# K and V read in 2 MB blocks instead of 1 MB blocks, in the first three passes of an attention and dense forward and backward kernel

## The chip, the cores and the metric

The kernel runs on one core of one Trainium2 chip. The metric is the time of one execution on the device, in microseconds (us); lower is better. The state of a run says whether it fell into a disturbed, slower execution. Medians are quoted with their range.

The engines are called as in the profile: PE multiplies matrices (PEld are its weight loads), DVE does vector work, ACT does activations and copies, POOL does general work and SP only issues DMA transfers here. A core has 16 DMA engines. PSUM is the memory that PE's results go to. The granted clock is the share of its full speed that PE was allowed, as the profile records it.

## The reference, cut to what matters

The program is one decode step (a single token) through two pairs of attention and dense layer, with the gradients of everything. The attention layers share one cache of keys and values.

```python
# Hq, Hkv, Sk, Dh = 32, 4, 65536, 128     k_cache, v_cache: 64 MB each, bfloat16
def _A_ref(x, k_cache, v_cache, wq, wo):
    q = ...(x @ wq)
    scores = einsum(q, k) * Dh ** -0.5
    p = softmax(scores); o = einsum(p, v)
    return o @ wo
def _B_ref(x, w1, b1, w2, b2):            # w1: 1024 x 3584, w2: 3584 x 1024
    h = relu(x @ w1 + b1); return (h * h) @ w2 + b2
x = x + _A_ref(_layernorm(x), ...); x = x + _B_ref(_layernorm(x), ...)   # twice
# outputs: x, and by jax.vjp the gradients of x, k_cache, v_cache, wq, wo, w1, b1, w2, b2
```

Almost all of the data is the cache. It is read in four passes: forward of the first attention layer, forward of the second, backward of the second, and a last pass that does the rest of the backward work and writes the two cache gradients.

## The kernel before, where the change and the argument touch it

The slots. K and V blocks, weight slabs and staging for stores share 12 buffers of 1 MB (later also the buffers of `E`, the exponentials of the scores). A slot is given back with a time stamp and the one given back longest ago is taken first. The clock of these stamps, `NOW["step"]`, is one per step of a pass, plus 0.01 for each slot given back. All of this happens while the program is built; on the chip only the result exists, as instructions that wait for the last readers of the slot they overwrite.

```python
BLK = J * DH                                   # J = 32 keys of 128 elements: 8 KB per partition
FREE = [(0, i) for i in range(NSLOT)]          # NSLOT = 12, kept sorted by time
NOW = {"step": 0}

class Slot:
    def __init__(self, name, fill=False):
        n = 0
        if fill:                               # used by stores and a few others
            ready = [k for k, (at, _) in enumerate(FREE) if at <= NOW["step"] - 1]
            n = ready[-1] if ready else 0
        self.i = FREE.pop(n)[1]
        ...

def give_slot(i, more=0):
    NOW["step"] += 0.01
    insort(FREE, (NOW["step"] + more, i))

def kv8(t, g, c8):                             # 8 columns of keys; loads their block at first touch
    b, j = divmod(c8, J)
    key = (t, g, b)
    if key not in KV["have"]:
        sl = Slot("blk_" + t)
        v = sl.t[:, :].rearrange("p (j d) -> p j d", d=DH)
        nc.sync.dma_start(out=v, in_=KVIN[t][g][b])
        KV["have"][key] = (sl, v)
    return KV["have"][key][1][:, j:j + 8, :]
```

Between two passes lies a dense stretch, in which layer weights stream through the same slots.

A forward pass. For each group of eight K columns, PE transposes them (`kT`), ACT or DVE copies the result out of PSUM as a K tile (`kt`), PE multiplies it with the query (`kS`), and after 128 columns ACT does eight exponentials. The V product follows 23 steps behind.

```python
def kT(g, c8):
    kb8 = kv8("k", g, c8)
    ...                                        # 8 transposes into PSUM
    evac(kt[:, :, :], pt[:, :, :])             # K tile: by ACT or DVE, whichever has less to do
def stats(g, su):                              # every 128 columns
    ...
    for h in range(R):                         # R = 8 exponentials on ACT
        nc.scalar.activation(out=E(g, c0, SU)[:, :, L["lr"].start + h], in_=S[:, h, :], func=ACTF.Exp, ...)
def v8(g, c8): ...                             # V product with E
FWD_LAG = TLEAD + SU // 8 + 5                  # TLEAD = 2, SU = 128
pipeline(items, [(kT, 0), (kS, TLEAD), (v8, FWD_LAG)], bg, end)
```

## Time and profile before

The median of three runs was 2037.67 us (2037.56 to 2038.18).

I cut the span into stages by the first and last matmul of each pass that reads a K or V block. The next fence is the view of time windows of the kernel before, one line for a stage: passes one, two, three and four are lines 1, 3, 5 and 7, and the dense stretches between them are lines 2, 4 and 6. Columns: window, its length, then busy us (and instructions) of PE, PEld, DVE, ACT and POOL, the granted clock of PE, the busy share of the 16 DMA engines, and GB/s.

```profile
12.50:377.90 365.40, 296.27 (x6656) 280.57 (x6657) 168.10 (x387) 175.40 (x387) 0.29 (x1) 0.93 1.01 411
377.90:433.30 55.40, 44.03 (x818) 42.43 (x815) 22.07 (x61) 13.68 (x15) 0.55 (x11) 0.85 0.87 328
433.30:781.00 347.70, 285.42 (x6586) 270.65 (x6584) 165.89 (x382) 173.71 (x385) 0.29 (x1) 0.93 1.01 407
781.00:833.30 52.30, 39.67 (x786) 36.66 (x784) 24.32 (x66) 18.09 (x23) 0.48 (x9) 0.85 0.87 330
833.30:1197.50 364.20, 296.44 (x6509) 265.68 (x6506) 170.96 (x327) 151.06 (x186) 0.67 (x1) 0.96 1.01 412
1197.50:1255.70 58.20, 51.56 (x932) 48.51 (x929) 41.40 (x105) 34.63 (x40) 0.48 (x10) 0.84 0.82 299
1255.70:2012.90 757.20, 663.08 (x8376) 393.38 (x8376) 581.20 (x1201) 526.81 (x1011) 85.25 (x158) 0.91 0.97 399
```

In the three first passes the DMA share is 1.01, while PE is busy about four fifths of the time and DVE and ACT less than half. So the loads set the pace there. In the dense stretches the share is still 0.82 to 0.87.

The next lines are two windows of 50 us inside passes one and three of the kernel before, the same columns. They show the rate of a full stretch, 410 to 417 GB/s in nearly all such windows.

```profile
150.00:200.00 50.00, 42.21 (x957) 39.91 (x955) 24.40 (x53) 25.23 (x53) 0.00 (x0) 0.93 1.01 416
1100.00:1150.00 50.00, 39.20 (x823) 35.19 (x822) 23.43 (x40) 21.57 (x30) 0.00 (x0) 0.93 1.02 414
```

```profile
SPq L351 <- PE ps_mv L397: 36.8, 15, 11.4
```

### The profile page before, as it was taken

The page shows a single profiled execution, that of the slowest core. Times are in us where ns is not written, and L with a number is a line of the kernel's source. Part 1 is how long each engine was busy: PE and PEld are TensorE (multiplying, and loading weights), DVE is VectorE, ACT ScalarE, POOL GpSimd, SP SyncE. Part 2 cuts the span into 40 slices and gives each one's busy share as a digit, 9 for nine tenths or more (in the row PEclk, how much of TensorE's full clock was granted, in tenths as well). Part 3 has the DMA queues.
Part 4 walks back from the last instruction along what each step waited for, and adds up shares of the span by engine and source line. Part 5 has one row for each costly group of instructions (what it writes and reads, how often), then busy time and mean ns, then how long its engine had stood idle before and what let it go on. Part 6 is the DMA issues. An engine that isn't in the chain of part 4 may idle for free.

```text
span 2035.9 us, 69009 instructions
## 1 busy us (share of the span) xinstructions
PE 1689.3 (83%) x30754; PEld 1344.3 (66%) x30754; DVE 1188.6 (58%) x2586; ACT 1103.0 (54%) x2063; POOL 92.4 (5%) x232
## 2 busy tenths in 40 slices
PE   7888887688788886887978888979988978898897
PEld 6778777688787776776867777545544545454454
DVE  4444454255444542555464446867967877687775
ACT  3544454255444542445354345767766766576675
POOL 0000000000000000000000000101101111010111
PEclk9999899799899996999999988988988998698898
DMA  9999999999999998999999986999999999999995
GB/s 384 416 410 414 413 414 415 360 335 406 411 414 413 413 415 323 398 415 410 416 412 414 416 338 231 375 424 393 422 424 424 423 423 404 423 415 423 423 371 212
DMA packets 136536, 803.50 MB, mean 395 GB/s; under 512 B 12448, under 2 KB 12462, under 8 KB 52398
## 3 DMA queue, kind: packets, MB, share of 16 engines
q1 hardware_dynamic: 112190, 633.39, 76.9%
q0 software_dynamic: 24048, 165.70, 19.6%
q8 instruction: 240, 3.93, 0.8%
q14 instruction: 58, 0.48, 0.1%
HBM read 633.35 MB, written 165.69 MB: 392 GB/s over the span
## 4 chain that ended last, share of the span: by engine, by line
PE 45%; DMA 28%; ACT 15%; DVE 8%; issue 4%; SPq 0%; ACTq 0%; POOLq 0%; DVEq 0%; POOL 0%
DMA blk_v<-in_A_v_cache_dram 13%; PE ps_tr L774 7%; ACT E L831 6%; DMA blk_k<-in_A_k_cache_dram 5%; PE ps_sc L792 5%; PE ps_tr L1026 4%; PE ps_gg L1074 4%; PE ps_acc L858 4%; ACT kt L150 4%; PE ps_tr L917 3%; DVE kt L153 3%; DMA out_dram<-og 3%; PE ps_gg L1139 2%; DMA out_dram<-gstk 2%; PE ps_mv L397 2%
## 5 line engine op out<-in xcount | busy, mean ns | idle before, releaser
L153 DVE COPY kt<-ps_tr 128x1024 bf16<-128x1024 bf16 x751 | 507.3, 687 | 340.6 <-PE ps_tr L774 145.4
L150 ACT COPY kt<-ps_tr 128x1024 bf16<-128x1024 bf16 x273 | 275.7, 1024 | 410.9 <-PE ps_tr L774 230.0
L774 PE MATMUL ps_tr<-ident_b,blk_k 128*128 128x128 bf16 x4096 | 297.3, 226 | 4.3 <-DMA blk_k<-in_A_k_cache_dram 3.3
L150 ACT CAST gstk<-ps_gg 128x512 bf16<-128x512 f32 x396 | 207.6, 600 | 99.7 <-PE ps_gg L1074 78.5
L150 ACT CAST gstv<-ps_gg 128x512 bf16<-128x512 f32 x379 | 199.2, 601 | 100.1 <-PE ps_gg L1074 99.2
L774 PEld LDWEIGHTS <-blk_k 128*128 128x128 bf16 x4096 | 249.5, 102 | 4.9 <-DMA blk_k<-in_A_k_cache_dram 3.8
L792 PE MATMUL ps_sc<-L_qpad,kt 128*128 128x64 bf16 (+7 forms) x4096 | 197.4, 194 | 52.8 <-DVE kt L153 38.8
L1074 PE MATMUL ps_gg<-GG,xt 64*128 64x512 bf16 x1024 | 211.5, 403 | 21.2 <-ACT gstk L150 11.0
L792 PEld LDWEIGHTS <-kt 128*128 128x128 bf16 x4096 | 158.8, 100 | 71.3 <-DVE kt L153 45.7
L858 PE MATMUL ps_acc<-E,blk_v 128*128 128x64 bf16 (+4 forms) x4096 | 177.6, 200 | 33.0 <-issue 10.9
L1026 PEld LDWEIGHTS <-blk_v 128*128 128x128 bf16 x2048 | 128.5, 103 | 108.0 <-issue 83.0
L1026 PE MATMUL ps_tr<-ident_b,blk_v 128*128 128x128 bf16 x2048 | 183.0, 230 | 20.1 <-DMA blk_v<-in_A_v_cache_dram 18.9
L858 PEld LDWEIGHTS <-blk_v 128*128 128x128 bf16 x4096 | 152.9, 103 | 36.4 <-issue 31.3
L831 ACT ACTIVATE E<-S_sb,L_negm 128x128 bf16<-128x128 f32 x256 | 150.4, 990 | 38.2 <-DVE L_negm L827 38.1
L1101 PEld LDWEIGHTS <-blk_k 128*128 128x128 bf16 x2048 | 84.3, 100 | 115.7 <-issue 87.0
L917 PE MATMUL ps_tr<-ident_b,blk_v 128*128 128x128 bf16 x2048 | 143.7, 224 | 14.3 <-DMA blk_v<-in_A_v_cache_dram 12.0
L917 PEld LDWEIGHTS <-blk_v 128*128 128x128 bf16 x2048 | 121.4, 100 | 31.1 <-DMA blk_v<-in_A_v_cache_dram 20.6
L1101 PE MATMUL ps_acc<-X,blk_k 128*128 128x64 bf16 (+3 forms) x2048 | 119.2, 196 | 23.0 <-DMA blk_k<-in_A_k_cache_dram 23.0
L831 ACT ACTIVATION_READ_ACCUMULATOR E<-S_sb,L_negm 128x1 f32 x256 | 123.5, 483 | 0.0
L937 PE MATMUL ps_sc<-dOpad,kt 128*128 128x64 bf16 (+7 forms) x2048 | 100.7, 194 | 26.6 <-ACT kt L150 15.5
L1055 PE MATMUL ps_sc<-DOB,kt 128*128 128x64 bf16 (+3 forms) x2048 | 111.3, 198 | 0.2 <-DVE kt L153 0.2
L153 DVE CAST gstv<-ps_gg 128x512 bf16<-128x512 f32 x133 | 90.0, 684 | 28.1 <-PE ps_gg L1074 27.7
(271 smaller groups left out, 2203.0 us busy)
## 6 DMA issues: line engine op xcount, KB each, us to landing
blk_k<-in_A_k_cache_dram SPq DMA_DIRECT2D x248, 1024.0 KB, 20.1
blk_v<-in_A_v_cache_dram SPq DMA_DIRECT2D x243, 1024.0 KB, 20.2
out_dram<-gstv POOLq DMA_DIRECT2D x64, 1024.0 KB, 13.1
out_dram<-gstk POOLq DMA_DIRECT2D x64, 1024.0 KB, 12.5
s_wq<-in_A_wq_dram SPq DMA_DIRECT2D x32, 1024.0 KB, 18.8
s_wo<-in_A_wo_dram SPq DMA_DIRECT2D x32, 1024.0 KB, 20.2
s_w<-in_B_w_dram SPq DMA_DIRECT2D x32, 896.0 KB, 7.8
out_dram<-og POOLq DMA_DIRECT2D x23, 1024.0 KB, 13.9
```

The costliest lines, as they stand in the source:

```text
L150: nc.scalar.copy(out=out, in_=in_)
L153: nc.vector.tensor_copy(out=out, in_=in_)
L774: nc.tensor.transpose(pt[:, i, :], kb8[:, i, :], ident_b[:, :])
L792: nc.tensor.matmul(state["ps_s"][:, s:s + w, :].rearrange("p a b -> p (a b)"), lhsT=kt[:, i, :], rhs=L["qpad"][:, g, 0:w, :].rearrange("p ...
L831: nc.scalar.activation(out=E(g, c0, SU)[:, :, L["lr"].start + h], in_=S[:, h, :], func=ACTF.Exp, bias=negm[:, g, su, h:h + 1], scale=SCALE ...
L858: nc.tensor.matmul(ps_o[:, 0:w, :], lhsT=vb8[:, i, :], rhs=E(g, c, w)[:, :, lr], start=(c % SU == 0), stop=(c % SU == SU - 1), skip_group_ ...
L917: nc.tensor.transpose(pt[:, i, :], vb8[:, i, :], ident_b[:, :])
L937: nc.tensor.matmul(state["ps_dp"][:, s:s + w, :].rearrange("p a b -> p (a b)"), lhsT=vt[:, i, :], rhs=dOpad[:, g, 0:w, :].rearrange("p a b ...
L1026: nc.tensor.transpose(pt[:, i, :], vb8[:, i, :], ident_b[:, :])
L1055: nc.tensor.matmul(state["ps_dp"][:, s:s + w, :].rearrange("p a b -> p (a b)"), lhsT=vt[:, i, :], rhs=DOB[:, g, 0:w, :].rearrange("p a b - ...
L1074: nc.tensor.matmul(pgs[h][:, :], lhsT=xt[64 * h:64 * h + 64, j1 // 8 + m, :], rhs=gg[64 * h:64 * h + 64, :, :].rearrange("p a b -> p (a b) ...
L1101: nc.tensor.matmul(ps_dq[:, 0:w, :].rearrange("p a b -> p (a b)"), lhsT=kb8[:, i, :], rhs=X[:, s:s + w, :].rearrange("p a b -> p (a b)"), ...
```

## The change

The intent: with 16 KB instead of 8 KB in a row per partition there are half as many descriptors, each of twice the size, so the 16 DMA engines should move more bytes in a full stretch. Two neighbouring 1 MB slots of one arena take one 2 MB load. The slots still come free and are still taken one by one for weights. So that pairs survive, a single slot is taken by preference where its neighbour is already in use: the key of a free slot is its time stamp, plus 3 where the neighbour is free.

```diff
-    SLOTS = [(slotp, "slot%d" % i) for i in range(NSLOT)]
-    FREE = [(0, i) for i in range(NSLOT)]
-    NOW = {"step": 0}
+    JW = 2 * J
+    ARENA = slotp.tile([P, NSLOT * BLK], BF, name="arena")
+    GRAN = [ARENA[:, i * BLK:(i + 1) * BLK] for i in range(NSLOT)]
+    FREE = {i: 0.0 for i in range(NSLOT)}
+    NOW = {"step": 0, "pairs": True}
+    def wide(i):
+        return ARENA[:, i * BLK:(i + 2) * BLK]
+    def take_pair():
+        both = [(max(FREE[i], FREE[i + 1]), i) for i in range(0, NSLOT, 2) if i in FREE and i + 1 in FREE]
+        if not both:
+            return None
+        i = min(both)[1]
+        ...
+    def take_one(fill):
+        by_age = sorted((t, i) for i, t in FREE.items())
+        if fill:
+            ...                                  # as before
+        elif NOW["pairs"]:
+            i = min((t + (3 if i < NSLOT and (i ^ 1) in FREE else 0), i) for t, i in by_age)[1]
+        else:
+            i = by_age[0][1]
+        ...
     def give_slot(i, more=0):
         NOW["step"] += 0.01
-        insort(FREE, (NOW["step"] + more, i))
+        FREE[i] = NOW["step"] + more
     def kv_views(ap):
-        return [ap[0, g].rearrange("(b p j) d -> b p j d", p=P, j=J) for g in range(G)]
+        return [ap[0, g].rearrange("(b p j) d -> b p j d", p=P, j=JW) for g in range(G)]
     def kv8(t, g, c8):
+            if NOW["pairs"] and hb % 2 == 0 and (t, g, hb + 1) not in have:
+                i = take_pair()
+            if i is None:
+                ...                              # one 1 MB half, as before
+            else:                                # one 2 MB load into both halves
+                ... nc.sync.dma_start(out=wide(i)..., in_=KVIN[t][g][hb // 2])
     # before the pipeline of each of the four passes:
+        NOW["pairs"] = p < 3
+        KV["halves"] = set(TOUCH[p][-4:])         # the last four blocks of a pass: two 1 MB loads
```

The stores of the last pass now go in 8 KB pieces at a distance of 16 KB.

More of the change, by code (lines that the diff above doesn't have):

```diff
@@ L240, with __init__ @@
     BLK = J * DH
-    SLOTS = [(slotp, "slot%d" % i) for i in range(NSLOT)]
-    FREE = [(0, i) for i in range(NSLOT)]
-    NOW = {"step": 0}
-    class Slot:
-        def __init__(self, name, fill=False):
-            n = 0
-            if fill:
-                ready = [k for k, (at, _) in enumerate(FREE) if at <= NOW["step"] - 1]
-                n = ready[-1] if ready else 0
-            self.i = FREE.pop(n)[1]
-            pool, tag = SLOTS[self.i]
-            self.t = pool.tile([P, BLK], BF, name=name, tag=tag)
+    JW = 2 * J
[10 more added lines that the diff above has]
+        i = min(both)[1]
+        del FREE[i], FREE[i + 1]
+        return i
+    def take_one(fill):
+        by_age = sorted((t, i) for i, t in FREE.items())
+        if fill:
+            ready = [i for t, i in by_age if t <= NOW["step"] - 1]
+            i = ready[-1] if ready else by_age[0][1]
+        elif NOW["pairs"]:
+            i = min((t + (3 if i < NSLOT and (i ^ 1) in FREE else 0), i) for t, i in by_age)[1]
+        else:
+            i = by_age[0][1]
+        del FREE[i]
+        return i
+    class Slot:
+        def __init__(self, name, fill=False, at=None):
+            self.i = take_one(fill) if at is None else at
+            self.t = GRAN[self.i]
         def free(self, stored=False):
@@ L260, in give_slot, with add_slot, half @@
         NOW["step"] += 0.01
-        insort(FREE, (NOW["step"] + more, i))
-    def add_slot(pool, tag):
-        SLOTS.append((pool, tag))
-        give_slot(len(SLOTS) - 1)
+        FREE[i] = NOW["step"] + more
+    def add_slot(view):
+        GRAN.append(view)
+        give_slot(len(GRAN) - 1)
     def kv_views(ap):
-        return [ap[0, g].rearrange("(b p j) d -> b p j d", p=P, j=J) for g in range(G)]
+        return [ap[0, g].rearrange("(b p j) d -> b p j d", p=P, j=JW) for g in range(G)]
     KVIN = {"k": kv_views(A_k_cache), "v": kv_views(A_v_cache)}
+    def half(views, g, hb):
+        return views[g][hb // 2][:, J * (hb % 2):J * (hb % 2) + J, :]
     GKv = kv_views(out_2)
     GVv = kv_views(out_3)
-    KV = {"have": {}, "keep": set()}
+    KV = {"have": {}, "keep": set(), "halves": set()}
     def kv8(t, g, c8):
-        b, j = divmod(c8, J)
-        key = (t, g, b)
-        if key not in KV["have"]:
-            sl = Slot("blk_" + t)
-            v = sl.t[:, :].rearrange("p (j d) -> p j d", d=DH)
-            nc.sync.dma_start(out=v, in_=KVIN[t][g][b])
-            KV["have"][key] = (sl, v)
-        return KV["have"][key][1][:, j:j + 8, :]
+        hb, j = divmod(c8, J)
+        key = (t, g, hb)
+        have = KV["have"]
+        if key not in have:
+            i = None
+            if NOW["pairs"] and hb % 2 == 0 and (t, g, hb + 1) not in have:
+                i = take_pair()
+            if i is None:
+                sl = Slot("blk_" + t)
+                nc.sync.dma_start(out=sl.t.rearrange("p (j d) -> p j d", d=DH), in_=half(KVIN[t], g, hb))
+                have[key] = sl
+            else:
+                for h in range(2):
+                    have[(t, g, hb + h)] = Slot("blk_" + t, at=i + h)
+                if key in KV["halves"]:
+                    for h in range(2):
+                        nc.sync.dma_start(out=GRAN[i + h].rearrange("p (j d) -> p j d", d=DH), in_=half(KVIN[t], g, hb + h))
+                else:
+                    nc.sync.dma_start(out=wide(i).rearrange("p (j d) -> p j d", d=DH), in_=KVIN[t][g][hb // 2])
+        return have[key].t.rearrange("p (j d) -> p j d", d=DH)[:, j:j + 8, :]
     def kv_done(t, g, c8):
@@ L289, in kv_done @@
         if c8 % J == J - 8 and key not in KV["keep"]:
-            KV["have"].pop(key)[0].free()
+            KV["have"].pop(key).free()
     def order_by_unit(desc, unit):
@@ L698, in E_done @@
         if c0 % EH == 0 and EH * R2 == BLK:
-            add_slot(epool, "E%d_%d" % (g, c0 // EH))
+            add_slot(ETILE[(g, c0 // EH)][:, :])
     def gsl(g):
@@ L967, in attn_bwd3 @@
         KV["keep"] = plan_keep(p)
+        NOW["pairs"] = p < 3
+        KV["halves"] = set(TOUCH[p][-4:])
         pipeline(items, [(vT, 0), (vS, TLEAD), (k8, B3_LAG)], bg, end)
@@ L1086, in dV8 @@
             if 2 * j0 < J:
-                outer16("gstv", GVv[g][b], "stv", state[("xe", g, b)], state[("GG", g, c8 // SU)][1], 2 * j0)
+                outer16("gstv", half(GVv, g, b), "stv", state[("xe", g, b)], state[("GG", g, c8 // SU)][1], 2 * j0)
         def k8(g, c8):
@@ L1109, in k8 @@
             if 2 * j0 >= J:
-                outer16("gstk", GKv[g][b], "stk", xt, state[("GG", g, su)][0], 2 * j0 - J)
+                outer16("gstk", half(GKv, g, b), "stk", xt, state[("GG", g, su)][0], 2 * j0 - J)
         KV["keep"] = plan_keep(p)
+        NOW["pairs"] = p < 3
+        KV["halves"] = set(TOUCH[p][-4:])
         pipeline(items, [(vT, 0), (vS, TLEAD), (dV8, DV_LAG), (k8, B4_LAG)], bg, end)
```

## The prediction

> **What bounds the kernel now.** In the first three passes (about 20 to 360, 430 to 765 and 850 to 1180 us) the 16 DMA engines are full: the table of 50 us windows shows a DMA share of 1.01 to 1.02 and 410 to 417 GB/s in nearly every window. PE is busy 38 to 43 us of each 50, DVE and ACT about half. The waits rarely name DMA (PE waited some 3 us for K in pass one, 12 us for V in pass three), so compute is only a few per cent faster than the loads. Landed data not yet used, counted from packets and matmuls, falls in pass two from about 9 to 3 blocks, so there too the loads are slower than compute. Pass four (1260 to 2000 us) moves 396 to 425 GB/s of mixed loads and stores; the dense stretches between passes have DMA shares of 0.6 to 0.9.
>
> **What the change does.** About 370 of the 491 cache loads of 1 MB lie in passes one to three. Nearly all become 2 MB loads whose descriptor is 16 KB instead of 8 KB. By the packet records of the trace a load packet of 2 KB takes 84 ns and one of 8 KB 309 ns at best (318 mean): about 36.6 ns per KB plus 9 ns fixed. A 16 KB packet should take about 602 ns at best where two of 8 KB take 618, if the descriptor isn't split: some 2%. Half of the semaphore packets (9 ns each) go too: 0.2%. The Trainium skill, "DMA: Bandwidth & Descriptors", section "Bandwidth", measures 425 GB/s on 16 MB transfers; this trace reads at about 415. So I estimate 415 to 422 GB/s, 1.7%, on about 940 us of streaming: 16 us.
>
> **What it adds.** A pair of slots is taken and refilled whole. With two streams about one more block each is held half used, and one more must land before the first matmul. Blocks in flight are now about 5 to 6, falling to 2.5 while weights are loaded; I expect some two fewer, so a few short dips of DMA share where weights break a pair. Pass four loads and stores 8 KB pieces at a 16 KB stride: the same packet sizes, no change expected. Compute, kept blocks, dense stretches and the last loads of a pass (still halves) stay.
>
> **On the critical path.** Loads set the pace of passes one and three nearly throughout, of pass two at its end only; compute stalls (exponentials of 4.7 us per 128 keys a row, evacuations) take over once the loads are 2 to 4% faster. I count 14 us of the 16 as won, and nothing lost to starvation in the centre. Predicted: 2023 us, range 2006 to 2038. Chances: faster by over 2% 0.07, within 2% 0.90, slower by over 2% 0.03.
>
> **What would show it.** Right: packets of 16 KB of about 600 to 620 ns; 420 to 425 GB/s in the windows of passes one to three; each 4 to 6 us shorter; pass four and dense stretches unchanged to a few us. Wrong step one: 16 KB packets cost twice the 8 KB ones or are split, so GB/s stay at 415. Step two: GB/s in full windows rise, but some windows drop below 0.97 share while the DMA queue waits for PE to release slots. Step three: DMA share drops evenly: compute is the limit.
>
> **What would make it wrong.** A stride of 16 KB that slows pass four; a slot order entering pass four that delays stores; waits on the shared arena coarser than on separate slots; HBM liking long rows more than the smaller packets show.

## More of the kernel before

The weight slabs.

The generator holds one slab at a time (`ahead=1`): it takes a slot and issues the load, hands out the slab, and frees the slot when the matmuls of that slab are in the program. Whether the next load can start early on the chip depends only on which slot it gets.

```python
def slabs(name, load, nk, kper, ncols, ahead=1):
    ...
    def fetch():
        ...
        sl = Slot(name)
        nc.sync.dma_start(out=v, in_=load(k, kn))
        pend.append((k, kn, sl, v))
    def gen():
        while ks or pend:
            while ks and len(pend) < ahead:
                fetch()
            k, kn, sl, v = pend.popleft()
            for kk in range(kn):
                yield k + kk, v[:, kk, :]
            sl.free()                          # NOW["step"] += 0.01, nothing else moves the clock here
```

The part of the page on DMA issues, kernel before: what is loaded, line's engine and kind, count, KB each, median us from issue to landing.

```profile
blk_k<-in_A_k_cache_dram SPq DMA_DIRECT2D x248, 1024.0 KB, 20.1
blk_v<-in_A_v_cache_dram SPq DMA_DIRECT2D x243, 1024.0 KB, 20.2
...
s_w<-in_B_w_dram SPq DMA_DIRECT2D x32, 896.0 KB, 7.8
...
s_w<-in_B_w_dram SPq DMA_DIRECT2D x21, 1024.0 KB, 11.4
```

Finally the first dense stretch of the kernel before, from three views: what PE waited for (columns: total us, times, longest), what the DMA queue of SP waited for, and the timeline of SP (columns: start, length, engine, line, what, count).

```profile
PE ps_mv L397 <- DMA s_w<-in_B_w_dram: 5.5, 4, 1.8
```

```profile
380.75 27.42 SPq L351 DMA_DIRECT2D s_w<-in_B_w_dram  x12
...
418.61 6.88 SPq L282 DMA_DIRECT2D blk_k<-in_A_k_cache_dram  x3
```

Twelve slab loads are issued within 27 us; PE waits for them for only 5.5 us in all; and about 15 us before pass two begins, at 418.6 us, the first of three K blocks is already asked for. This agrees with the row on overlap in the Trainium skill, "DMA: Bandwidth & Descriptors", section "Rules for kernel authors", which says to issue a transfer early and wait for it late.

## The result, and the profile after

The changed kernel took 2225.57 us median (2222.56 to 2229.54, four runs) against 2037.62. The ratio is 1.093, with a 95% interval of 1.091 to 1.095. A ratio here is the mean time of one kernel's fast runs over that of the other's of the same rounds, so it is not quite the ratio of the two medians. All results were correct.

The changed kernel is slower, clear of the noise. Its stages, by the same view of windows and the same cut:

```profile
18.50:398.30 379.80, 299.88 (x6595) 287.11 (x6593) 170.41 (x384) 174.88 (x386) 0.29 (x1) 0.88 0.95 391
398.30:501.30 103.00, 46.41 (x676) 44.44 (x672) 17.96 (x43) 10.39 (x11) 0.00 (x0) 0.64 0.40 147
501.30:889.00 387.70, 300.23 (x6730) 286.49 (x6727) 172.37 (x400) 177.07 (x389) 0.84 (x12) 0.91 0.91 371
889.00:983.90 94.90, 49.81 (x787) 44.91 (x783) 25.22 (x66) 18.38 (x23) 0.48 (x9) 0.62 0.55 195
983.90:1343.40 359.50, 293.17 (x6506) 268.54 (x6503) 171.22 (x327) 151.86 (x186) 0.67 (x1) 0.94 1.00 412
1343.40:1441.40 98.00, 66.40 (x932) 59.43 (x930) 42.53 (x105) 35.33 (x40) 0.48 (x10) 0.72 0.51 183
1441.40:2197.40 756.00, 669.80 (x8375) 395.28 (x8375) 583.09 (x1201) 526.73 (x1011) 85.56 (x158) 0.90 0.97 400
```

Set beside each other, in us (the differences are mine, from unrounded times, so a stage can be 0.1 us off the windows above; "start" is the time to the first matmul that reads a K block, and a tail of 23 us is the same in both):

| stage | start | pass 1 | dense | pass 2 | dense | pass 3 | dense | pass 4 |
|---|---|---|---|---|---|---|---|---|
| before | 12.5 | 365.4 | 55.3 | 347.8 | 52.3 | 364.2 | 58.1 | 757.3 |
| after | 18.5 | 379.8 | 103.0 | 387.7 | 94.9 | 359.6 | 97.9 | 756.1 |
| difference | +6.0 | +14.4 | +47.7 | +39.9 | +42.6 | -4.6 | +39.8 | -1.2 |

The three dense stretches lose 130 us, although the change was not meant for them. The two forward passes lose 54. Pass three, the only one that behaves as intended, wins 5. Where the loads are dense they are indeed faster: in windows of 50 us within the three passes whose DMA share is at least 1.00, the mean is 420 GB/s (413 to 426) against 414 (410 to 417) before. Two such windows of the changed kernel follow (the first from pass one, the last from pass three). But pass one also has windows such as the second, with a DMA share of 0.89, where the kernel before keeps 1.01 or 1.02 from slice to slice of the pass:

```profile
150.00:200.00 50.00, 38.08 (x828) 36.44 (x825) 21.44 (x49) 23.35 (x60) 0.00 (x0) 0.90 1.01 425
200.00:250.00 50.00, 39.86 (x831) 38.35 (x832) 21.58 (x48) 18.29 (x38) 0.00 (x0) 0.78 0.89 343
1100.00:1150.00 50.00, 39.37 (x852) 35.99 (x850) 24.02 (x50) 21.39 (x28) 0.00 (x0) 0.93 1.01 422
```

The DMA issues of the changed kernel. Of 491 loads of K and V of 1 MB, 358 have become 179 of 2 MB. The last two lines are the weights of the dense layers: they land sooner after issue than before (4.6 and 4.9 us against 7.8 and 11.4), which sounds good and isn't: little else is in the queue beside them.

```profile
arena<-in_A_k_cache_dram SPq DMA_DIRECT2D x93, 2048.0 KB, 17.3
arena<-in_A_v_cache_dram SPq DMA_DIRECT2D x86, 2048.0 KB, 18.2
...
arena<-in_B_w_dram SPq DMA_DIRECT2D x32, 896.0 KB, 4.6
arena<-in_B_w_dram SPq DMA_DIRECT2D x21, 1024.0 KB, 4.9
```

The packet records of the traces settle the first step of the prediction. A packet of a 16 KB row took 608 ns at least, 614 in the median and 626 in the mean. Two load packets of 8 KB of the kernel before took 614, 626 and 637. So a row of 16 KB is about 2% quicker by median or mean. The rows are not split: there are 128 records of 16 KB for each of the 179 loads.

### The first dense stretch after

The same three views as before, of the changed kernel: waits of the engines, waits of SP's queue, timeline of SP.

```profile
PE ps_mv L433 <- DMA arena<-in_B_w_dram: 52.4, 11, 7.8
DVE mv_junk L559 <- DMA arena<-in_B_w_dram: 37.8, 6, 7.7
```

```profile
SPq L387 <- DMA arena<-in_B_w_dram: 34.1, 7, 6.9
SPq L387 <- DVE mv_junk L559: 32.7, 6, 7.0
```

```profile
407.29 0.33 SPq L319 DMA_DIRECT2D arena<-in_A_k_cache_dram  x1
409.16 0.33 SPq L387 DMA_DIRECT2D arena<-in_B_w_dram  x1
409.58 0.41 SPq L319 DMA_DIRECT2D arena<-in_A_k_cache_dram  x1
418.12 83.46 SPq L387 DMA_DIRECT2D arena<-in_B_w_dram  x11
```

PE waits eleven times, 52.4 us in all, or 4.8 us each, which is what one weight load takes by the issue lines. DVE, which reads the slabs of w2, waits six times for 37.8. The added wait, 52.4 - 5.5 = 46.9 us, is the added time of this stretch, 47.7. SP, which before sent twelve slab loads in 27 us, now needs 83 us for eleven: before each one it waits for the DVE instruction or the matmul that still reads the slab before, or for that slab's own load. Load, read, load, read: the stream has lost all overlap. Two K loads of 2 MB for pass two do go out early, at 407 and 410 us, but behind them and the slabs the next K load goes out only at 533 us.

The loss doesn't end where my cut puts the end of the stretch. Pass two begins there with the first transpose of K, at 501.3 us, but the last slabs of the stretch are still to come: PE's first product of K with the query follows 24.6 us later, where the kernel before needs 1.4 us. In between PE waits twice for wq, 8.1 us in all, and the DMA engines move some 200 GB/s. Counted from that first product to its end, pass two takes 363.2 us against 346.5. So about 23 of its 39.9 us belong to the dense stretch.

The reason can be printed, because slots are chosen while the program is built. These are the slots of the weight slabs of this stretch (eight of w1, seven of w2, two of wq), from the building of both programs:

```
before: w1 0 4 5 8 10 0 4 5    w2 8 10 0 4 5 8 10     wq 0 4
after:  w1 7 9 10 10 10 10 10 10   w2 10 10 10 10 10 10 10   wq 10 10
```

The penalty of 3 in `take_one` is in steps. In a pass the clock gains one per step, so three steps of age outweigh it. In a dense stretch nothing moves the clock but 0.01 for a slot given back, so age hardly counts. The free slots at the fourth slab of w1, as (time stamp, slot), printed while the changed program is built at step 280.40:

```
(280.36, 6) (280.37, 8) (280.38, 7) (280.39, 9) (280.40, 10)
```

Five slots are free, and slot 6 was given back longest ago. But 6 and 7 are neighbours, and so are 8 and 9: with the penalty their keys are 283.36 to 283.39. Slot 10 has its neighbour in use, so its key is 280.40 and it wins, although the slab before has only just given it back. At the next slab it wins again, and so on to the end of the stretch. The four older slots stay idle, kept for the two pairs with which pass two begins.

### The forward passes after

What PE waited for in pass two, first the kernel before, then the changed one (columns as above):

```profile
PE ps_sc L792 <- DVE kt L153: 16.8, 12, 2.4
PE ps_sc L792 <- ACT kt L150: 5.7, 16, 1.8
```

```profile
PE ps_sc L828 <- ACT kt L150: 32.7, 22, 4.4
PE ps_sc L828 <- DVE kt L153: 1.8, 3, 0.9
```

PE waits 27 us longer for K tiles that ACT has to copy out of PSUM, though both engines do the same work as before. Its waits for the K tiles that DVE copies became 15 us shorter, so 12 us are left as the net change for K tiles. The granted clock of PE was lower too (0.88 against 0.93 in pass one), but PE's recorded busy time grew by only 3.6 us in that pass, of the 14.4 that it lost. One wait for ACT, from the timeline of the changed kernel. First ACT: the first and the last exponential of a row of eight, and the copy after it; then PE (the bracket gives the idle time before an instruction, and what ended it):

```profile
665.99 0.85 ACT L867 ACTIVATE E<-S_sb,L_negm 128x128 bf16<-128x128 f32 x1 [3.62 <-DVE L_negm L863]
...
669.61 0.99 ACT L867 ACTIVATE E<-S_sb,L_negm 128x128 bf16<-128x128 f32 x1
...
670.15 1.30 ACT L150 COPY kt<-ps_tr 128x1024 bf16<-128x1024 bf16 x1
```

```profile
665.62 1.51 PE L810 MATMUL ps_tr<-ident_b,arena 128*128 128x128 bf16 x24
671.51 0.49 PE L828 MATMUL ps_sc<-L_qpad,kt 128*128 128x64 bf16 x8 [4.37 <-ACT kt L150]
```

PE has its 24 transposes done at 667.1 us. ACT began a row of exponentials at 666.0 and copies the K tile only behind all eight, at 670.2; PE stands idle for 4.37 us. The Trainium skill, "Perfetto Trace Analysis", section "Tensor Engine Instruction (MATMUL, LD_WEIGHTS)", says that ACT is strictly first in, first out; this trace agrees: the copy begins at 670.15 us, after the eighth exponential has begun at 669.61, though its input had been ready for some 3 us.

So it matters in which order the two stand in ACT's program. This is the start of that order in the built programs (k a K tile, S a copy of scores, E an exponential):

```
before: kkkkSkkkSkEEEEEEEESkkkSkEEEEEEEEkSkkkSkEEEEEEEEkSkkkSkEEEEEEEEkSkkkSkEEEEEEEE ...
after:  kkkkSkkkSkEEEEEEEESkkkSEEEEEEEEkkSkkkSEEEEEEEEkkSkkkSEEEEEEkEEkSkkkSEEEEEEkEE ...
```

Each row of eight comes after an S. Before, a K tile stands between the two in 22 of the 32 rows (both forward passes together); after, in 3. PE's order has changed too: before it alternates about four groups of K with four of V, after it does about eight and eight. The source says nothing of either. The framework orders instructions at build time, and the sizes and slots of the loads are the only thing that changed for it; with pairs turned off (experiment 2) the old order of ACT comes back. That it does so by its own estimate of when loads land is my inference.

### The profile page after: what moved, and what is told of

Read it like the earlier page. It is cut to its first block, busy times and chain, and to the rows that moved or that the text cites. A ratio compares the mean times of both kernels' runs of the same rounds, so it can differ in the third digit from the quotient of the medians.

```text
span 2220.8 us, 68825 instructions
## 1 busy us (share of the span) xinstructions
PE 1744.3 (79%) x30754; PEld 1397.7 (63%) x30754; DVE 1198.0 (54%) x2586; ACT 1104.6 (50%) x2063; POOL 92.7 (4%) x232
## 4 chain that ended last, share of the span: by engine, by line
PE 45%; DMA 31%; ACT 14%; DVE 6%; issue 4%; SPq 0%; ACTq 0%; POOLq 0%; DVEq 0%
DMA arena<-in_A_v_cache_dram 13%; PE ps_tr L810 9%; DMA arena<-in_B_w_dram 7%; ACT E L867 6%; PE ps_sc L828 6%; PE ps_tr L1066 4%; PE ps_gg L1114 4%; PE ps_acc L894 4%; DMA out_dram<-arena 4%; ACT kt L150 3%; PE ps_mv L433 3%; PE ps_gg L1181 3%; ACT arena L150 2%; DMA arena<-in_A_wo_dram 2%; DMA E<-in_A_v_cache_dram 2%
## 5 line engine op out<-in xcount | busy, mean ns | idle before, releaser
L150 ACT CAST arena<-ps_gg 128x512 bf16<-128x512 f32 x715 | 375.9, 599 | 180.7 <-PE ps_gg L1114 148.7
L810 PE MATMUL ps_tr<-ident_b,arena 128*128 128x128 bf16 x4096 | 330.3, 233 | 5.9 <-issue 5.6
L828 PE MATMUL ps_sc<-L_qpad,kt 128*128 128x64 bf16 (+7 forms) x4096 | 217.2, 198 | 82.3 <-ACT kt L150 73.0
L810 PEld LDWEIGHTS <-arena 128*128 128x128 bf16 x4096 | 265.3, 105 | 8.4 <-issue 7.8
L153 DVE CAST arena<-ps_gg 128x512 bf16<-128x512 f32 x294 | 199.4, 687 | 87.4 <-PE ps_gg L1114 41.1
L828 PEld LDWEIGHTS <-kt 128*128 128x128 bf16 x4096 | 175.6, 102 | 95.2 <-ACT kt L150 81.3
L955 PE MATMUL ps_tr<-ident_b,arena 128*128 128x128 bf16 x2048 | 160.0, 230 | 32.6 <-DMA arena<-in_A_v_cache_dram 29.5
L894 PE MATMUL ps_acc<-E,arena 128*128 128x64 bf16 (+4 forms) x4096 | 158.5, 197 | 28.4 <-ACT L_fw L915 9.9
L1066 PE MATMUL ps_tr<-ident_b,arena 128*128 128x128 bf16 x1728 | 153.5, 230 | 13.5 <-DMA arena<-in_A_v_cache_dram 12.5
L894 PEld LDWEIGHTS <-arena 128*128 128x128 bf16 x4096 | 143.8, 101 | 31.2 <-issue 30.5
L1066 PEld LDWEIGHTS <-arena 128*128 128x128 bf16 x1728 | 108.0, 102 | 85.4 <-issue 67.5
L955 PEld LDWEIGHTS <-arena 128*128 128x128 bf16 x2048 | 128.6, 103 | 48.6 <-DMA arena<-in_A_v_cache_dram 43.9
L433 PEld LDWEIGHTS <-arena 128*128 128x128 bf16 x1920 | 87.3, 115 | 97.7 <-DMA arena<-in_B_w_dram 80.6
L150 ACT COPY wt<-ps_tr 128x1024 bf16<-128x1024 bf16 (+1 forms) x42 | 39.1, 953 | 174.2 <-PE ps_tr L568 161.4
L150 ACT CAST E<-ps_gg 128x512 bf16<-128x512 f32 (+1 forms) x197 | 104.5, 607 | 35.7 <-PE ps_gg L1114 31.2
L1141 PEld LDWEIGHTS <-arena 128*128 128x128 bf16 x1600 | 66.4, 101 | 83.5 <-issue 68.0
L975 PE MATMUL ps_sc<-dOpad,kt 128*128 128x64 bf16 (+7 forms) x2048 | 106.5, 194 | 14.1 <-ACT kt L150 6.5
```

Of the source, the lines that this page charges most:

```text
L150: nc.scalar.copy(out=out, in_=in_)
L153: nc.vector.tensor_copy(out=out, in_=in_)
L433: nc.tensor.matmul(ps[:, :, nb], lhsT=cols(slab, nb), rhs=xcol(kc).to_broadcast([P, rep]), start=first, stop=last, skip_group_check=True)
L810: nc.tensor.transpose(pt[:, i, :], kb8[:, i, :], ident_b[:, :])
L828: nc.tensor.matmul(state["ps_s"][:, s:s + w, :].rearrange("p a b -> p (a b)"), lhsT=kt[:, i, :], rhs=L["qpad"][:, g, 0:w, :].rearrange("p ...
L894: nc.tensor.matmul(ps_o[:, 0:w, :], lhsT=vb8[:, i, :], rhs=E(g, c, w)[:, :, lr], start=(c % SU == 0), stop=(c % SU == SU - 1), skip_group_ ...
```

## The experiments

Theory A: the rule for single slots, applied where its clock stands still, costs the three dense stretches. Theory B: the forward passes lose by ACT's order. Rivals for the forward passes: pairs broken by weight slabs, or less room because pairs come free late (the coarser grain of the loads); the longer distance that a pair needs between K and V; PE's order; the arena and its strides.

The runs were made in four groups, each with fresh runs of the kernel before on the same chip, whose medians were 2035.16, 2035.76, 2033.28 and 2037.01 us. Ratios are against those.

### Experiment 1 (e4_dense): the rule off between the passes

```diff
-    NOW = {"step": 0, "pairs": True}
+    NOW = {"step": 0, "pairs": False}
     # after each of the forward and the third pass:
+        NOW["pairs"] = False
```

> The kernel after, with the rule that spares whole pairs switched off between the passes, so weight slabs there rotate over the free slots again; passes as in the kernel after. Theory 'weight slots': dense stretches back to 52 to 62 us each, total 2226 minus about 131, 2080 to 2105 us; pass one stays near 380 and pass two near 388 us, for these have another cause. Rival 'pairs': dense stretches stay near 100 us, total over 2200.

Measured: 2082.94 us, ratio 1.0235 (1.0208 to 1.0263). The windows of e4_dense for the three dense stretches:

```profile
398.10:461.30 63.20, 45.40 (x847) 43.77 (x843) 22.42 (x63) 13.68 (x15) 0.55 (x11) 0.80 0.77 288
...
834.40:886.60 52.20, 38.90 (x787) 35.74 (x784) 24.29 (x66) 18.02 (x23) 0.48 (x9) 0.87 0.88 325
...
1247.70:1303.40 55.70, 48.79 (x932) 46.00 (x930) 41.21 (x104) 34.68 (x40) 0.48 (x10) 0.90 0.83 305
```

They fall from 103.0, 94.9 and 97.9 us to 63.2, 52.2 and 55.7: 125 us, and pass two gains 15 more, since its beginning no longer waits for slabs (its first K product comes 2.5 us after its first transpose). Three quarters of the loss is theory A, by an edit that touches no load of K or V. Pass one (378.0) and pass two (373.1) are still slow, so something else is there.

### Experiment 2 (e2_single): arena and strides, but never a pair

```diff
-        NOW["pairs"] = p < 3          # in all four passes
+        NOW["pairs"] = False
```

> The kernel after with pairing never allowed: one arena, 64 keys a partition, but every load a half of 8 KB rows at a 16 KB stride, slots taken oldest first. Theory 'slot choice and 2 MB grain': layout, stride and arena cost nothing, so 2030 to 2044 us, each stage within 4 us of the kernel before, and load windows at 410 to 417 GB/s. Rival 'layout' (a stride or coarser waits on the arena cost part of it): over 2050.

Measured: 2036.90 us, ratio 1.0004 (0.9986 to 1.0021). One arena, the views of 64 keys per partition and the 8 KB pieces at a distance of 16 KB cost nothing, in pass four neither (756.8 us). What costs anything in the changed kernel comes with the pairs.

### Experiment 3 (e3_serial): the cost of theory A put into the kernel before

```diff
+            if NOW["dense"] and name.startswith("s_w"):
+                n = -1                # the slot given back last
             self.i = FREE.pop(n)[1]
     # NOW["dense"]: True between the passes, False in them
```

> The kernel before (no pairs, no arena), with one thing changed: in the three dense stretches a weight slab takes the slot that was freed last instead of the one freed first, so all its slabs go through one slot. Theory 'weight slots' (the loss is weight loads that wait for the slab before them to be read): the dense stretches, 55, 52 and 58 us in the kernel before and 103, 95 and 98 us in the kernel after, lengthen to about 95 to 105 us each, the passes stay, total 2155 to 2180 us. Rival 'pairs' (the loss comes from 2 MB grains and from fewer free slots): nothing here is paired, so total within 10 us of 2037.

Measured: 2275.22 us, ratio 1.1176 (1.1149 to 1.1202). The mechanism is confirmed, since the kernel before loses in the same stretches without any pair; its waits in the first dense stretch have the same form, fourteen of 4.6 us:

```profile
PE ps_mv L399 <- DMA s_w<-in_B_w_dram: 63.8, 14, 6.8
```

The size was missed by about 100 us (by the ratio, 239 us were lost). My imitation is harsher than the original, which leaves a few slabs other slots: the stretches took 115, 132 and 139 us. Pass two also became 20 us longer, and for the same reason as in the changed kernel: its first K product comes 26 us after its first transpose, behind the last slabs. Counted from that product, it takes 342 us, no more than the 346.5 of the kernel before.

### Experiment 4 (e6_wpair): do weight slabs break pairs in the passes?

On e4_dense, a weight slab takes a whole pair and the next slab its other half, so no pair is broken.

```diff
-            sl = Slot(name)
+            at = held.popleft() if held else None
+            if at is None and NOW["pairs"]:
+                at = take_pair()
+                if at is not None:
+                    held.append(at + 1)
+            sl = Slot(name, at=at)
```

> As e4, lag 23 kept, but in the passes the two slabs of a weight group take the two halves of one pair, so one pair at a time is out of use instead of up to two. Theory 'broken pairs': passes one and two fall to 355 to 362 and 335 to 345 us, total 2020 to 2045. Theory 'burst': they stay within 8 us of e4, total 2075 to 2105.

Measured: 2085.60 us, ratio 1.0249 (1.0231 to 1.0267), the same as e4_dense. Broken pairs are not the reason. The prediction had expected its dips of the DMA share from just these.

### Experiment 5 (e5_lag27): more distance between K and V

On e4_dense, V follows four steps later.

```diff
-    FWD_LAG = TLEAD + SU // 8 + 5
+    FWD_LAG = TLEAD + SU // 8 + 9
```

> As e4, and in the two forward passes V follows K by 27 steps of 8 key columns instead of 23, so that a K pair and a V pair (8 steps each) come free 3 and 5 steps apart instead of 1 and 7. By the program's own list of slots this also makes the weights of a group use one pair at a time. Theory 'burst' (pairs of K and V released together leave the loads idle): pass one falls from about 380 to 355 to 362 us and pass two from about 388 to 335 to 345, total 2020 to 2045. Theory 'broken pairs' alone: the same here, told apart by e6. If neither is the cause, passes stay, total 2080 to 2105.

Measured: 2051.73 us, ratio 1.0091 (1.0069 to 1.0114): 31 us better than e4_dense, but short of what I expected. About two fifths of the loss (ratio 1.0091 of 1.0235) remained, so the distance was not the whole story. The order changed with it, as the trace shows: PE's groups of eight and eight became fewer, while ACT had a K tile ahead in only 2 of the 32 rows. Its control is the same edit on the kernel before (e7_lag27b):

> Control: the kernel before with the lag of V raised from 23 to 27 steps and nothing else. If the lag only matters with pairs ('burst'), 2035 to 2045 us: at most 3 us more in each of two passes for four more steps at the end. If the lag itself helps (the gain of e5 over e4 is no matter of pairs), 2000 to 2020.

Measured: 2035.62 us, ratio 0.9998 (0.9977 to 1.0019). Without pairs the distance is worth nothing.

### Experiment 6 (e8_ten and e9_aged): room and grain

If pairs cost by tying up slots, the kernel before should suffer from two slots fewer in its forward passes (e8_ten):

```diff
+        hidden = [FREE.pop(0), FREE.pop(0)]
         pipeline(items, [(kT, 0), (kS, TLEAD), (v8, FWD_LAG)], bg, end)
         st.close()
+        for h in hidden:
+            insort(FREE, h)
```

> The kernel before with single blocks, but only ten of the twelve slots in the two forward passes (two are set aside and given back at the end of each). Theory 'grain' (pairs keep about two blocks' room half used, so fewer blocks are in flight and the extra matrix products of a weight group leave the loads idle): passes one and two 8 to 20 us longer each with dips of the DMA share after the weight groups, total 2050 to 2075. If the room doesn't matter: within 5 us of the kernel before.

Measured: 2043.46 us, ratio 1.0029 (1.0006 to 1.0052). Two of twelve slots are worth 6 us there, not 46. The Trainium skill, "Perfetto Trace Analysis", section "Optimization Strategy", says that the same gap repeating on the engine that should be saturated can mean that there isn't enough room for the next tile. That would have fitted the picture, but this run doesn't support it. It tests room in the kernel before only; two slots fewer in the changed kernel were not tried.

And if it cost to wait until a fresh pair is really read, a pair should be taken only when both halves were given back at least twelve steps ago, and two single loads made otherwise (e9_aged, on e5_lag27):

```diff
-        i = min(both)[1]
+        at, i = min(both)
+        if at > NOW["step"] - 12:
+            return None
```

> As e5 (weights rotate between passes, lag 27), and a pair is taken whole only where both its halves were given back at least 12 steps before; else the block is loaded as a single of 1 MB. About 300 of 368 blocks stay wide by the program's own list. Theory 'grain': the dips behind the weight groups shrink, pass one 358 to 364, pass two 342 to 352, total 2025 to 2042. If the dips have nothing to do with the wait for whole pairs: 2048 to 2060, as e5.

Measured: 2053.74 us, ratio 1.0087 (1.0058 to 1.0115), no better than e5_lag27. Neither grain nor room had explained the loss.

### Experiment 7 (e10_ktfirst): ACT's old order, pairs kept

On e4_dense, each exponential gets an edge of order, without a semaphore, behind the copy of the newest K tile that ACT makes. The loads don't change, and PE's order in the built program stays in the main that of the changed kernel, eight and eight.

```diff
-            evac(kt[:, :, :], pt[:, :, :])
+            ev = evac(kt[:, :, :], pt[:, :, :])       # evac now returns ACT's instruction, or None for DVE
+            if ev is not None:
+                state["ev"] = (NOW["step"], ev)
     ...
-                nc.scalar.activation(...Exp...)
+                ex = nc.scalar.activation(...Exp...)
+                if "ev" in state and NOW["step"] - state["ev"][0] < 1.5:
+                    after(ex, state["ev"][1])          # order only
```

> As e4 (pairs, weights rotating between passes, lag 23). The built program shows that ACT's order changed with the pairs: in the forward passes 29 of 32 rows of eight exponentials (4.7 us) stand ahead of a K tile's evacuation that in the kernel before stands ahead of them in 22 of 32. Here the old order is imposed on ACT alone. Theory 'ACT order': PE's waits for ACT's K tiles fall from about 33 to under 8 us in pass two, passes one and two 10 to 20 us shorter each than in e4 (378, 373), total 2045 to 2065. Theory 'PE order' (K tiles and V products of a pair stand in runs of eight): little here, 2072 to 2090.

Measured: 2037.27 us, ratio 1.0018 (0.998 to 1.0056): 46 us better than e4_dense and more than I expected. A K tile now stands ahead in 25 of the 32 rows. Pass one and pass two of e10_ktfirst in the view of windows:

```profile
19.10:373.30 354.20, 284.24 (x6595) 270.36 (x6592) 169.70 (x384) 176.06 (x386) 0.29 (x1) 0.93 1.00 416
...
436.60:786.50 349.90, 285.12 (x6549) 272.36 (x6550) 167.75 (x380) 175.28 (x385) 0.29 (x1) 0.93 0.98 400
```

Pass one takes 354.2 us instead of 378.0 and reads at 416 GB/s with a DMA share of 1.00. The dips in the DMA share of pass one were thus a consequence of the order. SP's waits fit this: in e4_dense, between 60 and 385 us, SP waited 148 us for the transposes that still read the slot it wanted next, in e10_ktfirst, between 60 and 360 us, 100 us. So I read it thus: PE stood idle, gave slots back late, and the loads had nowhere to go. In pass two the wait for ACT's K tiles is back to about its old size (e10_ktfirst, waits):

```profile
PE ps_sc L833 <- ACT kt L150: 7.2, 15, 1.7
```

### Experiment 8 (e11_expfirst): the other order in the kernel before, 1 MB loads

```diff
+                if h == R - 1 and "ev" in state and NOW["step"] - state["ev"][0] < 1.5:
+                    after(state["ev"][1], ex)          # the K tile behind the eighth exponential
```

> The kernel before, single blocks of 1 MB, with one edge for each row of exponentials: the K tile's evacuation that ACT has next goes behind the eight exponentials instead of ahead of them (32 of 32 rows, against 10 of 32); PE keeps runs of four. Theory 'ACT order': passes one and two 8 to 20 us longer each than 365 and 348, total 2050 to 2075, PE's waits for ACT's K tiles well above the 9 us of each pass. If the order costs only together with 2 MB loads: within 6 us of the kernel before.

Measured: 2098.17 us, ratio 1.0295 (1.0281 to 1.031). Passes one and two lose 30 and 35 us, more than the 8 to 20 that I expected of each, with the loads as they were and PE still mostly in its pattern of four and four. The wait from the changed kernel appears in it (e11_expfirst, waits in pass two):

```profile
PE ps_sc L797 <- ACT kt L150: 29.4, 22, 3.8
PE ps_acc L865 <- ACT E L836: 22.9, 5, 6.2
```

Taking the order away gains 46 us and adding it loses 61, the second with all 32 rows and not 29. Theory B is shown from both sides; that the loss was larger than expected is not explained.

### Experiment 9 (e13_weave, e14_clump, e15_both): PE's order

e13_weave forces PE on e4_dense to the old pattern of four groups of K and four of V, by the same kind of edge between transposes and V products:

```diff
+            if n % WEAVE == 0 and n + FWD_LAG < len(Ts):        # WEAVE = 4
+                for x in ins:
+                    after(x, Ts[n + FWD_LAG][7])
+            if n % WEAVE == WEAVE - 1:
+                ...                                             # the next transposes after this V product
```

> As e4, with PE's order in the forward passes imposed as it is in the kernel before: four key tiles transposed, then four V products, instead of eight and eight; loads are still pairs. Theory 'PE order': the evacuations again have V products to hide behind, passes one and two 12 to 25 us shorter each than in e4, load windows at 418 to 425 GB/s without dips, total 2025 to 2050. If grain of the slots is the cause, the order changes nothing: 2072 to 2090, or longer, because PE now waits for data.

Measured: 2083.50 us, ratio 1.0241 (1.0197 to 1.0284), the same as e4_dense. PE's old order alone gives nothing back. PE's wait for ACT's K tiles fell to 18.9 us in pass two without any gain in time, so that wait marks the order but doesn't measure its cost.

e14_clump puts the pattern of eight and eight into the kernel before (the same edit with WEAVE = 8):

> The kernel before, single blocks of 1 MB, with the order of the kernel after imposed on PE in the forward passes: eight key tiles transposed, then eight V products. Theory 'PE order': passes one and two 12 to 25 us longer each (365, 348 before), total 2058 to 2085. Theory 'grain of the slots' (2 MB loads are needed for the loss): within 6 us of the kernel before.

Measured: 2058.80 us, ratio 1.0113 (1.0078 to 1.0149). This one is confounded. When I looked at the built program, ACT's order had changed with it: only 5 of the 32 rows had a K tile ahead. It can't be told which of the two cost the 25 us.

e15_both is e13_weave with the edit of e10_ktfirst:

> e13 and e10 together: pairs, weights rotating, PE and ACT both in the order of the kernel before. If the loss in the forward passes is the order and nothing else, the gain of the longer rows shows: pass one 358 to 364, pass two 338 to 346, pass three near 361, total 2015 to 2035. If something of the 2 MB grain remains: 2040 to 2065.

Measured: 2056.29 us, ratio 1.0101 (1.0065 to 1.0137). I expected the best kernel of all and got one that is 19 us worse than e10_ktfirst with its one edit. Why both old orders together are worse than one is open; that forcing an order by edges does harm of its own would be a guess.

### Experiment 10 (e17_afterkt): only ACT's order undone

The changed kernel with the edit of e10_ktfirst and nothing else, so theory A's cost stays in.

> The kernel after, as it is, with ACT's order of e10 alone; weight slabs still go through the slot freed last between the passes. If the two causes add, e10's gain over e4 (about 46 us) comes off the 2226: 2170 to 2190, dense stretches still 95 to 105 us each, passes one and two near 356 and 350 to 360.

Measured: 2186.25 us, ratio 1.073 (1.0702 to 1.0758), as expected. Order alone is worth 39 us where the dense stretches are slow and 46 where they are not; the slot rule alone is worth 143 (2225.57 to 2082.94) or 149 (2186.25 to 2037.27). Undone alone, the two give 39 and 143 us, which adds up to the whole loss of 188 within 6 us. The slot rule's part is larger than the 125 us of the stretches by the beginning of pass two: here that pass takes 373.4 us against 349.9 in e10_ktfirst, but counted from its first K product 347.9 against 347.6.

### Experiment 11 (e12_lag27kt, e16_agedkt): a version that is better than both

e12_lag27kt has the flag off between passes, ACT's old order, and four steps more between K and V: the edits of e4_dense, e10_ktfirst and e5_lag27 together.

> e10 with V 27 steps behind K instead of 23. Passes one and two with ACT's old order gained all but 2 us of their time in e10; with lag 27 the first dense stretch was 55 us in e5 against 63. If both add: pass one 354 to 360, dense stretch one 55 to 58, pass two 342 to 350, total 2022 to 2034, below the kernel before. If e10 had already all there is: 2034 to 2042.

Measured over five rounds: 2025.99 us (2022.86 to 2027.97), ratio 0.9943 (0.9931 to 0.9956). It beats the kernel before by 0.6%, and is the fastest of all. Pass one of e12_lag27kt in the view of windows:

```profile
18.50:373.70 355.20, 295.34 (x6595) 281.85 (x6593) 171.39 (x384) 176.67 (x386) 0.29 (x1) 0.91 1.00 416
```

e16_agedkt adds the rule of e9_aged, in the hope of winning the late start back:

> e12 with the rule of e9: a pair is taken whole only when both halves came back 12 steps before, else a single block. With the order mended, if waiting for whole pairs costs something at the start of a pass and behind the weight groups, this is faster than e12 by 3 to 10 us, 2018 to 2030; if not, it loses a part of the wide loads (about 300 of 368 stay) and is slower by 1 to 4 us.

Measured: 2033.32 us, ratio 0.9979 (0.9967 to 0.9992). The start is indeed 12.5 us again, but with fewer 2 MB loads pass one takes 363.3 us instead of 355.2. It isn't worth it.

## Why the prediction was wrong, point by point

- **What bounds the kernel** was read rightly: the loads. e10_ktfirst and e12_lag27kt, which undo the two accidents, read at 416 GB/s in pass one against 411, and that pass takes 354 and 355 us against 365. But the margin of compute was so thin that a mere change of order made it the limit (e11_expfirst, with the loads as they were).
- **Step one, the larger rows,** was right in mechanism and about right in size. I predicted 602 ns at best for a 16 KB packet; the least was 608 and the median 614. (My own figures, 309 ns for 8 KB of which 9 are fixed, give 2 x 309 - 9 = 609, so the 602 does not follow from them.) Predicted were 420 to 425 GB/s in full windows; 413 to 426 were seen, 420 in the mean, or 1.6% more than before. In e12_lag27kt, which undoes both accidents but also has the longer distance and the forced order, pass one gains 10.2 us and pass three 2.8, but pass two only 0.2 and the start loses 6, because a first block of 2 MB lands later. So of the 14 us that I counted, 7 were to be had in these four, and some 10 to 12 in all (9.7 between the two traces; the ratio of the runs is 0.9943).
- **The step that failed** is in "What it adds": "Compute, kept blocks, dense stretches and the last loads of a pass (still halves) stay." Two of these did not stay.
  - The dense stretches did not stay: 130 us by the stage table, and some 23 us more in the beginning of pass two; undoing the rule alone wins 143 us. Their slabs take slots by the rule that was written for pairs. I had read that rule in the diff and asked only what it does in a pass. It showed in the source: `ahead=1` allows overlap only through a different slot, the penalty is 3, and the clock moves by 0.01.
  - Compute did not stay: 39 to 46 us. The instructions are the same, but the order on ACT is not. It showed nowhere in the diff, but listing ACT's order in the built program shows it without any run.
- **"Nothing lost to starvation in the centre"** was wrong in size. The dips of the DMA share that I expected "where weights break a pair" did come, but e6_wpair shows that broken pairs are not their reason, and e10_ktfirst removes them by ACT's order.
- **What would make it wrong.** The stride, and waits on the shared arena coarser than on slots: refuted by e2_single (ratio 1.0004). A "slot order entering pass four that delays stores" was the nearest guess, that slots could be chosen badly; but pass four kept its time (756.1 against 757.3), and the bad choice lay in the stretches before it.
- **The range** of 32 us was far too narrow for a change that rewrites the allocator of everything in the program. It priced the loads that the change is about, and left 0.03 for slower by over 2%.

What stays open: why e15_both is worse than e10_ktfirst; what e5_lag27 gains, since ACT's order in e13_weave is almost the same and gains nothing; and by what rule the framework chose the new order.

## What to carry to other kernels

A rule that weighs two things in units of a clock must be tried in every stage that uses it: here a penalty of three steps meets a stage in which the clock gains a hundredth per event, and a stream that overlapped loading with reading turns into load, read, load, read. When a change of load sizes slows compute that it doesn't touch, list the order of each engine's instructions in both built programs before thinking of the hardware; here five experiments went to other theories first. And a buffer that lands faster than before can be a bad sign: it had the queue for itself.

## What the Trainium skill lacked or had wrong

- "DMA: Bandwidth & Descriptors", section "Bandwidth": it measures 341 GB/s, 78%, for a transfer of 1 MB and 425 for 16 MB, and advises at least 1 MiB. The table is for transfers issued from GpSimd. Here SP issues them, and with a queue kept full 1 MB loads already ran at 410 to 417 GB/s and 2 MB loads at 413 to 426, so the gain from doubling is some 2%, far less than the table suggests.
- The same section gives no time for a packet of 8 or 16 KB. The packet records of loads in the changed kernel show medians of 309 ns for 8 KB and 614 ns for 16 KB; in the kernel before 8 KB took 313. So the fixed part of a packet is only some nanoseconds at these sizes, by estimate 2 x 309 - 614 = 4 ns, 12 with the 313, or about 9 from the 2 KB packets in the prediction.
- "Perfetto Trace Analysis", section "DMA Optimizations", says that larger DMA sizes saturate bandwidth better. That held in full windows (414 against 420 GB/s in the mean), and the program was still 9.3% slower. The page doesn't say that the size of loads can change the order of compute instructions (46 us here), nor that the slots of the larger loads can take the overlap away from others (130 us).
- "Perfetto Trace Analysis", section "Optimization Strategy", offers missing room as what repeating bubbles can mean. Two slots of twelve fewer cost the kernel before 6 us (e8_ten), while the order within one strictly ordered engine cost 46 and, in e11_expfirst, 61. The section doesn't name the order of an engine's queue as a cause of repeating gaps.
